# Squeeze-and-excitation scaling of a 256 x 256 x 384 image: more rows kept in SBUF, another row layout, small loads at the end of the first pass, a quartered first store, and an early table load

## Chip, cores, metric

One core of a Trainium2 chip. Times are device microseconds (us) of one execution; medians over several executions are given. Kernel before: 315.64 us median of 4 runs (315.46 to 316.08).

## The reference

```python
def reference(x, w_down, w_up):          # x: 1 x 256 x 256 x 384, bf16
    s = x.mean(axis=(1, 2))
    s = _sigmoid(_silu(s @ w_down) @ w_up)
    return x * s[:, None, None, :]
```

The scale of every channel depends on all pixels, so x has to be read once for the mean and be there a second time for the product. x is 50.3 MB and SBUF is smaller: what doesn't fit is loaded twice. Below, "row" is one pixel's 384 channels, 768 bytes in each of 128 partitions, that is 98,304 bytes in all; x has 512 rows per partition.

## The kernel before

```python
    R = 16; budget = 207_500; misc_bytes = 5 * 1024        # [defaults written in; cut]
    S = min(T, (budget - misc_bytes) // slot_bytes)         # 16 slots of 16 rows
    xv = xf.rearrange("(t p r) c -> t p (r c)", p=P, r=R)   # a tile is one contiguous block
    # ... [cut]
    for t in range(T):                                      # pass 1
        xt = slots[t % S]
        nc.sync.dma_start(out=xt[:, :], in_=xv[t])
        accumulate_rows(xt, R)          # one matmul with a column of ones per row, into sum_ps
    # mean_sb (ACT) -> psT (PE) -> sT_b (DVE) -> z_ps (PE) -> sig_sb (ACT) -> silu_sb (DVE)
    # -> z2_ps (PE) -> s_bc (ACT): the scale row in all partitions   [cut]
    # pass 2: for each tile in the queue, the resident ones first:
    nc.vector.tensor_tensor(out=x3, in0=x3, in1=s_bc[...], op=ALU.mult)   # in place
    nc.scalar.dma_start(out=dst, in_=xs_)
    nc.sync.dma_start(out=slots[v][:, :], in_=xv[nt])       # the slot's next tile, if any left
```

Loads go through the SP queue, stores through the ACT queue. The tile framework puts in the waits: a load into a slot waits for those stores that read the bytes it overwrites.

Of the kernel before, what the change touches and what calls it, by code (L numbers as in the profile page):

```python
# [10 lines left out]
BF16 = mybir.dt.bfloat16  # L11
ACT = mybir.ActivationFunctionType
ALU = mybir.AluOpType

_D = lambda k, d: type(d)(os.environ.get(k, str(d)))


@with_exitstack
def kernel(
    ctx: ExitStack,  # L20
    tc: tile.TileContext,
    x: bass.AP,
    w_down: bass.AP,
    w_up: bass.AP,
    out: bass.AP,
):
    nc = tc.nc
    P = nc.NUM_PARTITIONS

    B, H, W, C = x.shape  # L30
    Cr = w_down.shape[1]
    NROWS = B * H * W
    assert C % P == 0
    KC = C // P

    xf = x.rearrange("b h w c -> (b h w) c")
    of = out.rearrange("b h w c -> (b h w) c")

    ROW_BYTES = C * 2

    R = _D("DEV_R", 16)
    budget = _D("DEV_BUDGET", 207_500)
    misc_bytes = 5 * 1024
    p1_load_eng = _D("DEV_P1L", "sync")
    p2_load_eng = _D("DEV_P2L", "sync")
    p2_store_eng = _D("DEV_P2ST", "scalar")
    tail_split = _D("DEV_TAIL", 1)
    first_split = _D("DEV_FIRST", 1)
    nfree = _D("DEV_NFREE", 0)

    rows_pp = NROWS // P
    while R > 1 and rows_pp % R != 0:
        R //= 2
    T = rows_pp // R
    slot_bytes = R * ROW_BYTES
    S = min(T, (budget - misc_bytes) // slot_bytes)
    assert S >= 2, f"{S=}"
    n_res = S - nfree
    res_start = T - n_res
    if os.environ.get("DEV_VERBOSE", "1"):  # L60
        print(f"[dev] R={R} T={T} S={S} n_res={n_res} slot_bytes={slot_bytes} traffic_MB={(2*rows_pp+R*res_start)*ROW_BYTES*P/1e6:.1f}")

    xv = xf.rearrange("(t p r) c -> t p (r c)", p=P, r=R)
    ov = of.rearrange("(t p r) c -> t p (r c)", p=P, r=R)

    _engs = {"sync": nc.sync, "scalar": nc.scalar, "gpsimd": nc.gpsimd}

    def eng(name, i=0):
        if name in _engs:
            return _engs[name]  # L70
        if name == "alt":
            return nc.sync if i % 2 == 0 else nc.scalar
        if name == "alt3":
            return [nc.sync, nc.scalar, nc.gpsimd][i % 3]
        raise ValueError(name)

    consts = ctx.enter_context(tc.tile_pool(name="consts", bufs=1))
    small = ctx.enter_context(tc.tile_pool(name="small", bufs=1))
    slots_pool = ctx.enter_context(tc.tile_pool(name="slots", bufs=1))
    psum = ctx.enter_context(tc.tile_pool(name="psum", bufs=1, space=bass.MemoryType.PSUM))  # L80

    ones_bf = consts.tile([P, 1], BF16)
    nc.vector.memset(ones_bf[:], 1.0)  # L83
    ones_row = consts.tile([1, P], BF16)
    nc.vector.memset(ones_row[:], 1.0)  # L85

    wd_bf = consts.tile([P, KC, Cr], BF16)
    nc.scalar.dma_start(wd_bf[:], w_down.rearrange("(k p) j -> p k j", p=P))
    wu_bf = consts.tile([Cr, C], BF16)
    nc.scalar.dma_start(wu_bf[:], w_up)  # L90

    slots = [
        slots_pool.tile([P, R * C], BF16, tag=f"slot{v}", name=f"slot{v}") for v in range(S)
    ]

    sum_ps = psum.tile([1, C], FP32)
    total_mm = rows_pp
    mm_state = {"i": 0}

    def accumulate_rows(xt_ap, nrows):  # L100
        for r in range(nrows):
            i = mm_state["i"]
            nc.tensor.matmul(  # L103
                sum_ps[:, :],
                lhsT=ones_bf[:, 0:1],
                rhs=xt_ap[:, r * C : (r + 1) * C],
                start=(i == 0),
                stop=(i == total_mm - 1),
            )
            mm_state["i"] = i + 1  # L110

    for t in range(T):
        xt = slots[t % S]
        eng(p1_load_eng, t).dma_start(out=xt[:, :], in_=xv[t])  # L114
        accumulate_rows(xt, R)
    assert mm_state["i"] == total_mm

    mean_sb = small.tile([1, C], BF16)
    nc.scalar.activation(mean_sb[:], sum_ps[:], ACT.Copy, scale=1.0 / float(NROWS))  # L119
    psT = psum.tile([P, KC * P], FP32)  # L120
    for k in range(KC):
        nc.tensor.matmul(  # L122
            psT[:, k * P : (k + 1) * P],
            lhsT=mean_sb[0:1, k * P : (k + 1) * P],
            rhs=ones_row[0:1, 0:P],
            start=True,
            stop=True,
        )
    sT_b = small.tile([P, KC * P], BF16)
    nc.vector.tensor_copy(sT_b[:], psT[:])  # L130
    z_ps = psum.tile([Cr, P], FP32)
    for k in range(KC):
        nc.tensor.matmul(  # L133
            z_ps[:, :],
            lhsT=wd_bf[:, k, :],
            rhs=sT_b[:, k * P : (k + 1) * P],
            start=(k == 0),
            stop=(k == KC - 1),
        )
    sig_sb = small.tile([Cr, P], BF16)  # L140
    nc.scalar.activation(sig_sb[:], z_ps[:], ACT.Sigmoid)  # L141
    silu_sb = small.tile([Cr, P], BF16)
    nc.vector.tensor_mul(silu_sb[:], z_ps[:], sig_sb[:])  # L143
    z2_ps = psum.tile([P, C], FP32)
    nc.tensor.matmul(  # L145
        z2_ps[:, :], lhsT=silu_sb[:, :], rhs=wu_bf[:, :], start=True, stop=True
    )
    s_bc = small.tile([P, C], BF16)
    nc.scalar.activation(s_bc[:], z2_ps[:], ACT.Sigmoid)  # L149

    store_state = {"i": 0}

    def scale_and_store(xt, dst, parts=1):
        assert R % parts == 0
        rp = R // parts
        for q in range(parts):
            xs_ = xt[:, q * rp * C : (q + 1) * rp * C]
            x3 = xs_.rearrange("p (r c) -> p r c", c=C)
            nc.vector.tensor_tensor(  # L159
                out=x3,  # L160
                in0=x3,
                in1=s_bc[:, None, :].to_broadcast([P, rp, C]),
                op=ALU.mult,
            )
            eng(p2_store_eng, store_state["i"]).dma_start(  # L165
                out=dst[:, q * rp * C : (q + 1) * rp * C], in_=xs_
            )
            store_state["i"] += 1

    pending = []  # L170
    load_i = 0
    reload = list(range(res_start))
    free_slots = [v for v in range(S) if not (T - 1 - ((T - 1 - v) % S)) >= res_start]
    last_occ = {}
    for t in range(T):
        last_occ[t % S] = t
    free_slots = [v for v in range(S) if last_occ[v] < res_start]
    order = []
    rq = 0
    for v in free_slots:  # L180
        if rq < len(reload):
            tt = reload[rq]
            rq += 1
            eng(p2_load_eng, load_i).dma_start(out=slots[v][:, :], in_=xv[tt])
            load_i += 1
            pending.append((tt, v))
    resident = sorted((t, v) for v, t in last_occ.items() if t >= res_start)
    queue = list(resident) + list(pending)
    pending = []
    qi = 0  # L190
    while qi < len(queue):
        tt, v = queue[qi]
        qi += 1
        is_last = (qi == len(queue)) and rq >= len(reload)
        parts = 1
        if qi == 1:
            parts = first_split
        if is_last or (rq >= len(reload) and qi > len(queue) - 1):
            parts = tail_split
        scale_and_store(slots[v], ov[tt], parts=parts)  # L200
        if rq < len(reload):
            nt = reload[rq]
            rq += 1
            eng(p2_load_eng, load_i).dma_start(out=slots[v][:, :], in_=xv[nt])
            load_i += 1
            queue.append((nt, v))


# [28 lines left out]
```

## Time and profile before

| | before |
|---|---|
| time | 315.64 us |
| HBM read / written | 75.53 / 50.33 MB |
| DMA rate when full | 426 GB/s in pass 1, 430 in pass 2 |
| last load landed to first store's bytes | 123.5 to 134.0 us |
| VectorE, TensorE busy | 34%, 29% |

VectorE and TensorE are far from full. What bounds the kernel, and the lines that show it, stand in the prediction.

### The profile page before, as it was taken

The numbers are of one execution on the slowest core, as the hardware profiler recorded it, in microseconds if no ns is written. First come the engines' busy times: TensorE is split into PE (matmuls) and PEld (weight loads), VectorE is DVE, ScalarE is ACT, GpSimd is POOL, SyncE is SP. The second block draws the span as 40 slices with busy tenths as digits, with TensorE's granted clock in tenths as the row PEclk, the third lists the DMA queues.
The fourth block names the chain that finished last, engine by engine and source line by source line (L and its number), as shares of the span: only waits on it lengthen the run. The fifth ranks groups of instructions, "written<-read, shape, count | busy, mean of one in ns | idle before, by whom it ended". The sixth has DMA issues, their size and how long they took to land.

```text
span 314.0 us, 1303 instructions
## 1 busy us (share of the span) xinstructions
PE 91.7 (29%) x519; PEld 44.0 (14%) x519; DVE 106.5 (34%) x36; ACT 3.8 (1%) x5; POOL 0.2 (0%) x4
## 2 busy tenths in 40 slices
PE   0977577777777777200000000000000000000000
PEld 0433233333333333000000000000000000000000
DVE  0000000000000000599999999994444444000000
ACT  1000000000000000300000000000000000000000
POOL 0000000000000000000000000000000000000000
PEclk9999999999999999655555555555555555555555
DMA  7999999999999994099999999999999999999997
GB/s 284 425 426 423 427 424 426 423 427 426 426 425 427 426 426 184 0 376 343 431 427 429 431 434 431 429 427 429 429 434 431 429 427 431 428 434 431 429 427 307
DMA packets 11962, 125.95 MB, mean 401 GB/s; under 512 B 1692, under 2 KB 1716, under 8 KB 1716
## 3 DMA queue, kind: packets, MB, share of 16 engines
q1 hardware_dynamic: 6912, 75.50, 57.3%
q10 hardware_dynamic: 5044, 50.37, 38.0%
q8 instruction: 4, 0.07, 0.1%
q14 instruction: 2, 0.02, 0.0%
HBM read 75.53 MB, written 50.33 MB: 401 GB/s over the span
## 4 chain that ended last, share of the span: by engine, by line
DMA 76%; DVE 6%; PE 1%; ACT 0%; issue 0%; SPq 0%; ACTq 0%; DVEq 0%
DMA slot<-in_x_dram 38%; DMA out_dram<-slot 34%; DVE slot L159 5%; DMA wd_bf<-in_w_down_dram 5%; PE sum_ps L103 1%; DVE sT_b L130 0%; PE z_ps L145 0%; ACT s_bc L149 0%; ACT mean_sb L119 0%; SPq L114 0%; PE psT L122 0%; PE z_ps L133 0%; DVE silu_sb L143 0%; ACT sig_sb L141 0%; ACTq L165 0%
## 5 line engine op out<-in xcount | busy, mean ns | idle before, releaser
L159 DVE TENSOR_TENSOR slot<-slot,s_bc 128x6144 bf16<-128x6144 bf16 x32 | 105.4, 3357 | 29.7 <-DMA slot<-in_x_dram 28.6
L103 PE MATMUL sum_ps<-slot,ones_bf 128*1 128x384 bf16 x512 | 90.5, 332 | 35.8 <-DMA slot<-in_x_dram 35.8
L103 PEld LDWEIGHTS <-ones_bf 128*1 128x1 bf16 x512 | 43.5, 85 | 82.4 <-issue 44.9
L130 DVE CAST sT_b<-psT 128x384 bf16<-128x384 f32 x1 | 0.6, 559 | 126.2 <-PE psT L122 126.2
L119 ACT ACTIVATE mean_sb<-sum_ps 1x384 bf16<-1x384 f32 x1 | 0.5, 480 | 123.1 <-PE sum_ps L103 123.1
L119 ACT ACT_TABLE_LOAD x1 | 1.3, 1283 | 2.0 <-issue 2.0
L141 ACT ACT_TABLE_LOAD x1 | 1.3, 1283 | 0.0
L145 PE MATMUL z_ps<-wu_bf,silu_sb 24*128 24x384 bf16 x1 | 0.5, 496 | 0.7 <-DVE silu_sb L143 0.7
L143 DVE TENSOR_TENSOR silu_sb<-z_ps,sig_sb 24x128 bf16<-24x128 f32 x1 | 0.3, 278 | 0.7 <-ACT sig_sb L141 0.7
L133 PE MATMUL z_ps<-sT_b,wd_bf 128*24 128x128 bf16 x3 | 0.3, 217 | 0.7 <-DVE sT_b L130 0.7
L122 PE MATMUL psT<-ones_row,mean_sb 1*128 1x128 bf16 x3 | 0.3, 218 | 0.6 <-ACT mean_sb L119 0.6
L149 ACT ACTIVATE s_bc<-z_ps 128x384 bf16<-128x384 f32 x1 | 0.5, 491 | 0.9 <-PE z_ps L145 0.9
L133 PEld LDWEIGHTS <-wd_bf 128*24 128x24 bf16 x3 | 0.2, 90 | 0.7 <-issue 0.6
L83 DVE MEMSET ones_bf<- 128x1 bf16 x1 | 0.1, 59 | 0.8 <-PEq L221 0.8
L122 PEld LDWEIGHTS <-mean_sb 1*128 1x128 bf16 x3 | 0.2, 93 | 1.0 <-ACT mean_sb L119 1.0
L141 ACT ACTIVATE sig_sb<-z_ps 24x128 bf16<-24x128 f32 x1 | 0.3, 267 | 0.1
L145 PEld LDWEIGHTS <-silu_sb 24*128 24x128 bf16 x1 | 0.1, 98 | 0.8 <-DVE silu_sb L143 0.8
L85 DVE MEMSET ones_row<- 1x128 bf16 x1 | 0.2, 165 | 0.0
L221 POOL MEMSET const-bfloat16-1.0<- 128x1 bf16 x1 | 0.1, 102 | 0.0
L221 POOL MEMSET const-uint8-127<- 128x1 uint8 x1 | 0.1, 102 | 0.0
L221 POOL MEMSET const-float32-0.0<- 128x1 f32 x1 | 0.1, 99 | 0.2 <-issue 0.2
L221 POOL MEMSET const-float32-1.0<- 128x1 f32 x1 | 0.1, 99 | 0.0
## 6 DMA issues: line engine op xcount, KB each, us to landing
slot<-in_x_dram SPq DMA_DIRECT2D x48, 1536.0 KB, 25.5
out_dram<-slot ACTq DMA_DIRECT2D x32, 1536.0 KB, 29.0
wd_bf<-in_w_down_dram ACTq DMA_DIRECT2D x1, 18.0 KB, 14.4
wu_bf<-in_w_up_dram ACTq DMA_DIRECT2D x1, 18.0 KB
```

The source lines that it names most:

```text
L85: nc.vector.memset(ones_row[:], 1.0)
L103: nc.tensor.matmul(sum_ps[:, :], lhsT=ones_bf[:, 0:1], rhs=xt_ap[:, r * C : (r + 1) * C], start=(i == 0), stop=(i == total_mm - 1),)
L119: nc.scalar.activation(mean_sb[:], sum_ps[:], ACT.Copy, scale=1.0 / float(NROWS))
L122: nc.tensor.matmul(psT[:, k * P : (k + 1) * P], lhsT=mean_sb[0:1, k * P : (k + 1) * P], rhs=ones_row[0:1, 0:P], start=True, stop=True,)
L130: nc.vector.tensor_copy(sT_b[:], psT[:])
L133: nc.tensor.matmul(z_ps[:, :], lhsT=wd_bf[:, k, :], rhs=sT_b[:, k * P : (k + 1) * P], start=(k == 0), stop=(k == KC - 1),)
L141: nc.scalar.activation(sig_sb[:], z_ps[:], ACT.Sigmoid)
L143: nc.vector.tensor_mul(silu_sb[:], z_ps[:], sig_sb[:])
L145: nc.tensor.matmul(z2_ps[:, :], lhsT=silu_sb[:, :], rhs=wu_bf[:, :], start=True, stop=True)
L149: nc.scalar.activation(s_bc[:], z2_ps[:], ACT.Sigmoid)
L159: nc.vector.tensor_tensor(out=x3, in0=x3, in1=s_bc[:, None, :].to_broadcast([P, rp, C]), op=ALU.mult,)
L221: nc = _bacc.Bacc("TRN2", target_bir_lowering=False, num_devices=1)
```

## The change

Its intent: keep more of x in SBUF (18 slots of 16 rows and one of 3, so that 221 rows and not 256 are loaded twice), and shorten the gap between the passes from both sides. The core of the diff:

```diff
-    budget = _D("DEV_BUDGET", 207_500)
-    misc_bytes = 5 * 1024
+    budget = _D("DEV_BUDGET", 228224)
+    misc_bytes = _D("DEV_MISC", 4224)
-    first_split = _D("DEV_FIRST", 1)
+    first_split = _D("DEV_FIRST", 4)
+    slot_rows = [R] * n_full + ([extra_rows] if extra_rows else [])    # 18 x 16, 3
+    reload_tiles = [8] + [R] * nfr + [rem - 8]                         # 8, 13 x 16, 5
-    xv = xf.rearrange("(t p r) c -> t p (r c)", p=P, r=R)
+    xpp = xf.rearrange("(p r) c -> p (r c)", p=P)     # a partition owns 512 rows in sequence
+    if prewarm:
+        warm = consts.tile([1, 8], BF16)
+        nc.vector.memset(warm[:], 0.0)
+        nc.scalar.activation(warm[:], warm[:], ACT.Sigmoid)
+        if k == len(tiles) - 1:                       # pass 1, how a tile's load is cut
+            cut = [nr] if nr < 15 else [4, 4, 4, 2, 1]
+        elif k >= len(tiles) - 3:
+            cut = [4, 4, 4, 4]
+        for pi, rt in enumerate(pending_reload):      # pass 2, after a slot's store
+            if rt["nrows"] <= slot_rows[v]:
+                xr = slots[v][:, 0 : rt["nrows"] * C]
+                eng(p2_load_eng, load_i).dma_start(out=xr, in_=xpp[...])
-    nc = _bacc.Bacc("TRN2", target_bir_lowering=False, num_devices=1)
+    nc = _bacc.Bacc("TRN2", target_bir_lowering=False, num_devices=1, dynamic_dma_scratch_size=512)
```

The first tile to be loaded again has 8 rows, and it goes into rows 0 to 7 of slot 0, the slot whose multiply and store are made in four pieces of 4 rows.

More of the change, by code (lines that the diff above doesn't have):

```diff
@@ L32 @@
     NROWS = B * H * W
+    assert NROWS % P == 0
     assert C % P == 0
@@ L39 @@
     ROW_BYTES = C * 2
+    rows_pp = NROWS // P
     R = _D("DEV_R", 16)
-    budget = _D("DEV_BUDGET", 207_500)
-    misc_bytes = 5 * 1024
+    budget = _D("DEV_BUDGET", 228224)
+    misc_bytes = _D("DEV_MISC", 4224)
     p1_load_eng = _D("DEV_P1L", "sync")
@@ L47 @@
     tail_split = _D("DEV_TAIL", 1)
-    first_split = _D("DEV_FIRST", 1)
-    nfree = _D("DEV_NFREE", 0)
-    rows_pp = NROWS // P
-    while R > 1 and rows_pp % R != 0:
-        R //= 2
-    T = rows_pp // R
-    slot_bytes = R * ROW_BYTES
-    S = min(T, (budget - misc_bytes) // slot_bytes)
-    assert S >= 2, f"{S=}"
-    n_res = S - nfree
-    res_start = T - n_res
+    first_split = _D("DEV_FIRST", 4)
+    prewarm = _D("DEV_PREWARM", 1)
+    use_extra = _D("DEV_EXTRA", 1)
+    avail = budget - misc_bytes
+    n_full = min(avail // (R * ROW_BYTES), rows_pp // R)
+    extra_rows = 0
+    if use_extra:
+        extra_rows = (avail - n_full * R * ROW_BYTES) // ROW_BYTES
+        extra_rows = min(extra_rows, R - 1, rows_pp - n_full * R)
+        if extra_rows < 1:
+            extra_rows = 0
+    slot_rows = [R] * n_full + ([extra_rows] if extra_rows else [])
+    S = len(slot_rows)
+    res_rows = sum(slot_rows)
+    assert res_rows <= rows_pp
+    reload_rows = rows_pp - res_rows
+    reload_tiles = []
+    nfr = reload_rows // R
+    rem = reload_rows - nfr * R
+    reload_tiles = [8] + [R] * nfr + [rem - 8]
+    assert rem > 8 and sum(reload_tiles) == reload_rows
+    tiles = []
+    row = 0
+    rr_slot = 0
+    for k, nr in enumerate(reload_tiles):
+        if nr <= 0:
+            continue
+        if nr < R and extra_rows and nr <= extra_rows:
+            v = n_full
+        else:
+            v = rr_slot % n_full
+            rr_slot += 1
+        tiles.append(dict(row=row, nrows=nr, resident=False, slot=v))
+        row += nr
+    for v in range(S):
+        nr = slot_rows[v]
+        tiles.append(dict(row=row, nrows=nr, resident=True, slot=v))
+        row += nr
+    assert row == rows_pp
     if os.environ.get("DEV_VERBOSE", "1"):
-        print(f"[dev] R={R} T={T} S={S} n_res={n_res} slot_bytes={slot_bytes} traffic_MB={(2*rows_pp+R*res_start)*ROW_BYTES*P/1e6:.1f}")
-    xv = xf.rearrange("(t p r) c -> t p (r c)", p=P, r=R)
-    ov = of.rearrange("(t p r) c -> t p (r c)", p=P, r=R)
+        print(f"[dev] R={R} S={S} slot_rows={slot_rows} res_rows={res_rows}/{rows_pp} reload_tiles={reload_tiles} traffic_MB={(2*rows_pp+reload_rows)*ROW_BYTES*P/1e6:.2f}")
+    xpp = xf.rearrange("(p r) c -> p (r c)", p=P)
+    opp = of.rearrange("(p r) c -> p (r c)", p=P)
     _engs = {"sync": nc.sync, "scalar": nc.scalar, "gpsimd": nc.gpsimd}
@@ L90 @@
     nc.scalar.dma_start(wu_bf[:], w_up)
+    if prewarm:
+        warm = consts.tile([1, 8], BF16)
+        nc.vector.memset(warm[:], 0.0)
+        nc.scalar.activation(warm[:], warm[:], ACT.Sigmoid)
     slots = [
-        slots_pool.tile([P, R * C], BF16, tag=f"slot{v}", name=f"slot{v}") for v in range(S)
+        slots_pool.tile([P, slot_rows[v] * C], BF16, tag=f"slot{v}", name=f"slot{v}")
+        for v in range(S)
     ]
@@ L110, in accumulate_rows @@
             mm_state["i"] = i + 1
-    for t in range(T):
-        xt = slots[t % S]
-        eng(p1_load_eng, t).dma_start(out=xt[:, :], in_=xv[t])
-        accumulate_rows(xt, R)
+    for k, t in enumerate(tiles):
+        nr = t["nrows"]
+        cut = [nr]
+        if k == len(tiles) - 1:
+            cut = [nr] if nr < 15 else [4, 4, 4, 2, 1]
+        elif k >= len(tiles) - 3:
+            cut = [4, 4, 4, 4]
+        assert sum(cut) == nr
+        r0 = 0
+        for cr in cut:
+            xt = slots[t["slot"]][:, r0 * C : (r0 + cr) * C]
+            eng(p1_load_eng, k).dma_start(
+                out=xt,
+                in_=xpp[:, (t["row"] + r0) * C : (t["row"] + r0 + cr) * C],
+            )
+            accumulate_rows(xt, cr)
+            r0 += cr
     assert mm_state["i"] == total_mm
@@ L151, with scale_and_store @@
     store_state = {"i": 0}
-    def scale_and_store(xt, dst, parts=1):
-        assert R % parts == 0
-        rp = R // parts
+    def scale_and_store(xt, nrows, dst, parts=1):
+        parts = max(1, min(parts, nrows))
+        base = nrows // parts
+        extra = nrows - base * parts
+        r0 = 0
         for q in range(parts):
-            xs_ = xt[:, q * rp * C : (q + 1) * rp * C]
+            rp = base + (1 if q < extra else 0)
+            if rp == 0:
+                continue
+            xs_ = xt[:, r0 * C : (r0 + rp) * C]
             x3 = xs_.rearrange("p (r c) -> p r c", c=C)
@@ L165, in scale_and_store @@
             eng(p2_store_eng, store_state["i"]).dma_start(
-                out=dst[:, q * rp * C : (q + 1) * rp * C], in_=xs_
+                out=dst[:, r0 * C : (r0 + rp) * C], in_=xs_
             )
             store_state["i"] += 1
-    pending = []
-    load_i = 0
-    reload = list(range(res_start))
-    free_slots = [v for v in range(S) if not (T - 1 - ((T - 1 - v) % S)) >= res_start]
-    last_occ = {}
-    for t in range(T):
-        last_occ[t % S] = t
-    free_slots = [v for v in range(S) if last_occ[v] < res_start]
@@ L178 @@
-    order = []
-    rq = 0
-    for v in free_slots:
-        if rq < len(reload):
-            tt = reload[rq]
-            rq += 1
-            eng(p2_load_eng, load_i).dma_start(out=slots[v][:, :], in_=xv[tt])
-            load_i += 1
-            pending.append((tt, v))
-    resident = sorted((t, v) for v, t in last_occ.items() if t >= res_start)
-    queue = list(resident) + list(pending)
-    pending = []
+            r0 += rp
+    resident = [t for t in tiles if t["resident"]]
+    reload = [t for t in tiles if not t["resident"]]
@@ L190 @@
+    queue = [(t, t["slot"]) for t in resident]
+    pending_reload = list(reload)
+    load_i = 0
     qi = 0
+    total = len(tiles)
+    n_done = 0
     while qi < len(queue):
-        tt, v = queue[qi]
+        t, v = queue[qi]
         qi += 1
-        is_last = (qi == len(queue)) and rq >= len(reload)
+        n_done += 1
+        is_last = n_done == total
         parts = 1
-        if qi == 1:
+        if qi <= 1:
             parts = first_split
-        if is_last or (rq >= len(reload) and qi > len(queue) - 1):
+        if is_last:
@@ L199 @@
             parts = tail_split
-        scale_and_store(slots[v], ov[tt], parts=parts)
-        if rq < len(reload):
-            nt = reload[rq]
-            rq += 1
-            eng(p2_load_eng, load_i).dma_start(out=slots[v][:, :], in_=xv[nt])
-            load_i += 1
-            queue.append((nt, v))
+        nr = t["nrows"]
+        xt = slots[v][:, 0 : nr * C]
+        scale_and_store(xt, nr, opp[:, t["row"] * C : (t["row"] + nr) * C], parts=parts)
+        for pi, rt in enumerate(pending_reload):
+            if rt["nrows"] <= slot_rows[v]:
+                pending_reload.pop(pi)
+                xr = slots[v][:, 0 : rt["nrows"] * C]
+                eng(p2_load_eng, load_i).dma_start(
+                    out=xr, in_=xpp[:, rt["row"] * C : (rt["row"] + rt["nrows"]) * C]
+                )
+                load_i += 1
+                queue.append((rt, v))
+                break
@@ L210 @@
+    assert not pending_reload, pending_reload
 _INS = ['x', 'w_down', 'w_up']
```

## The prediction

> **What bounds the kernel now.** The kernel walks x twice: pass 1 loads all 32 tiles of 1536 KB and sums them over the pixels on TensorE, a short chain turns the sums into the scale row s_bc, and pass 2 multiplies by it and stores; the last 16 tiles stay in SBUF and the first 16 are loaded again. I read first the busy share of the 40 slices, then the DMA totals:
>
> ```profile
> DMA  7999999999999994099999999999999999999997
> GB/s 284 425 426 423 427 424 426 423 427 426 426 425 427 426 426 184 0 376 343 431 427 429 431 434 431 429 427 429 429 434 431 429 427 431 428 434 431 429 427 307
> DMA packets 11962, 125.95 MB, mean 401 GB/s; under 512 B 1692, under 2 KB 1716, under 8 KB 1716
> ```
>
> The DMA engines are full everywhere but in three places: the first slice, the slices around 0 between the passes, and two slices just after. So time goes when bytes go, or when those holes shrink. Second, the stretch view, cut where the rate changes (columns: stretch, length, busy of PE, PEld, DVE, ACT, POOL, granted clock, DMA share, GB/s):
>
> ```profile
> 120.00:120.50 0.50, 0.50 (x4) 0.25 (x3) 0.00 (x0) 0.00 (x0) 0.00 (x0) 1.00 0.99 418
> 120.50:121.00 0.50, 0.50 (x5) 0.25 (x3) 0.00 (x0) 0.00 (x0) 0.00 (x0) 1.00 0.71 270
> 121.00:122.00 1.00, 1.00 (x9) 0.52 (x7) 0.00 (x0) 0.00 (x0) 0.00 (x0) 1.00 0.26 111
> 122.00:123.00 1.00, 0.63 (x4) 0.23 (x3) 0.00 (x0) 0.00 (x0) 0.00 (x0) 1.00 0.09 37
> 123.00:134.00 11.00, 3.92 (x23) 1.75 (x22) 4.92 (x4) 2.52 (x4) 0.00 (x0) 0.75 0.00 0
> 134.00:138.00 4.00, 0.00 (x0) 0.00 (x0) 4.00 (x2) 0.00 (x0) 0.00 (x0) 0.50 1.00 418
> 138.00:141.00 3.00, 0.00 (x0) 0.00 (x0) 3.00 (x2) 0.00 (x0) 0.00 (x0) 0.50 1.12 426
> 141.00:147.00 6.00, 0.00 (x0) 0.00 (x0) 6.00 (x3) 0.00 (x0) 0.00 (x0) 0.50 0.94 291
> 147.00:200.00 53.00, 0.00 (x0) 0.00 (x0) 53.00 (x17) 0.00 (x0) 0.00 (x0) 0.50 1.01 430
> ```
>
> Full rate ends near 121; then a few of the 16 DMA engines are still behind (share 0.26, then 0.09, one or two engines); from 123 to 134 nothing moves; stores begin at 134.0, and once loads join them a dip to 291 GB/s costs 6 x (430 - 291) / 430 = 1.9 us. After that 430 GB/s to the end. Third, the chain of work that ended last, in order of time (start, length, what), for the hole itself:
>
> ```profile
> 123.55 2.77 PE sum_ps L103 x16
> ...
> 126.35 0.49 ACT mean_sb L119
> ...
> 128.23 0.28 ACT sig_sb L141
> ...
> 129.40 0.50 ACT s_bc L149
> 129.90 0.02 issue
> 129.92 13.18 DVE slot L159 x4
> ```
>
> Between landing and first store lie 16 matmuls, 2.8 us; mean to scale row, 3.6 us; one multiply, 3.36 us; and 0.7 us from the issue of the store (133.31) to its first bytes (134.0). The end is no place to gain: VectorE makes its last multiply at 260.58, and the stores behind it drain at 430 GB/s for another 48 us.
>
> **What the Trainium skill says.** (1) "DMA: Bandwidth & Descriptors", section "Where 436 GB/s comes from", puts the ceiling of the 16 DMA engines at 435 GB/s; the 426 and 430 here agree, so no better queueing raises the plateau, only fewer bytes help. (2) "SBUF — State Buffer", section "SBUF size: 192, 224, or 256?", gives 224 KiB per partition, about 208 KiB after a reserve of 16 KiB for descriptors that software generates. Kernel before budgets 207,500 B; the change shrinks that reserve to 512 B and budgets 228,224. The page's DMA queues are hardware-dynamic ones and instruction ones, so the reserve serves nothing here; the trace shows nothing against it. (3) The first page again, section "Latency and other measured facts": copies of 128 partitions x 16 KiB lose rate when the row pitch in HBM is a large power of two, 207 GB/s per direction at 512 KiB against 214 at full, 164 at 2 MiB. No run so far shows this: the kernel before reads contiguous tiles.
>
> **The change, part by part.**
>
> *More kept in SBUF.* 228,224 - 4,224 = 224,000 B hold 18 slots of 12,288 B (before 16) and 2,816 B over, so one more slot of 3 rows. Resident are 18 x 16 + 3 = 291 rows per partition of 512, and 221 are loaded again in place of 256. 35 rows x 768 B x 128 partitions = 3.44 MB; at 430 GB/s that is 8.0 us. All of it lies on the bound resource, so it counts in full: -8.0 us.
>
> *The last loads of pass 1 cut small.* The last two full tiles come in pieces of 4 rows, the last piece has 3. After the last landing there are 3 matmuls and not 16: the 16 took 2.77 us, about 0.17 us each, so some 0.6 us, -2.2 us. The pieces before it land every 0.9 us and need 0.7 us of TensorE, so none pile up. The lagging DMA engines are not helped: each piece still needs all 16. Smaller packets cost: in the packet records 12,288 B take 460 ns and 768 B 36 ns; a line through them gives 7.7 ns plus 0.0368 ns per byte, so 3,072 B take 121 ns, and four of them 483 ns instead of 460. For 35 rows so cut that is 0.4 us, and for the split store 0.2: +0.6 us.
>
> *First multiply and store in four.* The first store can leave after a quarter of a multiply. A 128x6144 one takes 3.36 us, of which 6144 elements at 2 x 0.96 per ns are 3.2, so a quarter takes an estimated 0.95 us. Measured from s_bc ready, bytes start at 0.95 + 0.7 = 1.7 us rather than 4.05. But what comes next? Four quarters keep VectorE till 3.8, the next full multiply till 7.2, and the second tile's bytes start at 7.9. The first tile's bytes are through at 1.7 + 3.8 = 5.5. The first load of pass 2 waits for that store's landing (0.9 us after its bytes, as 137.7 to 138.6 before) and needs about 1.3 us to first bytes (as at the kernel's start, 0.73 to 2.0): 7.7. So a hole opens from 5.5 to 7.7. Before, the first tile's bytes were through at 4.05 + 3.7 = 7.7 and the second's ready at 7.4. Both kernels have moved one tile at 7.7 us: the head start of 2.3 us is given back, 0 us net.
>
> *Sigmoid's table loaded early.* The table load before sig_sb ran from 126.84 to 128.12, while z_ps came at 128.21: it was hidden by 0.1 us. 0 us.
>
> *Layout.* Each partition now owns 512 consecutive rows, so the 128 runs of one DMA lie 512 x 768 B = 384 KiB apart. Runs are still 12,288 B, so the packets stay the same size. 384 KiB is three times a power of two and smaller than the skill's mildest case of 3%; I book 0.2%, +0.5 us.
>
> Sum: 315.6 - 8.0 - 2.2 + 0.6 + 0.5 = 306.5 us.
>
> **The rivals.** *A: the pitch bites.* Streams 384 KiB apart might share HBM channels. For it: the skill's table, in which 512 KiB costs 3%; DMA engines in step at such pitches are just what this layout makes. Against it: pass 1 only reads, and the factor 3 spreads addresses. At 3% on 290 us the loss is 9 us and the kernel stands at 314, the same; at 1%, 309. *B: the quartered store does pay.* If the dip after 141 comes from stores and loads meeting with a backlog, then an early, lightly loaded start may remove it, or the load may arrive sooner than 7.7: up to 2.3 us more, 304. Against it stands the count above: VectorE delivers 1.57 MB in 3.36 us, 468 GB/s, too little more than 430 to refill a hole. *C: full slots or new waits.* Loads in flight at once are eight (the chain of waits goes in steps of 29.45 us, eight tiles of 3.68), and eight pieces of 4 rows hold only 7.4 us of work, so a late landing could starve the queue at the end of pass 1. The piece's wait is on a landing 8 DMAs back, and 2.3 us of lag plus 1.3 us of start still fit in 7.4: I give it at most 1 us, 307.5.
>
> **Range and chances.** The 8.0 and 2.2 us are counts on a bound stage, known to perhaps 0.5 us. B pulls to 303.5, A to 311 or, at a full 3%, to 314. So 306.5, range 303.5 to 311.0. Faster by over 2% means below 309.3; only A at more than 1% prevents that, which I give about one in five. Slower needs a pitch loss of 6%: 3%.
>
> **What would show it.** Right: bytes read fall by 3.44 MB; the plateau stays at 424 to 431 GB/s in both passes; three matmuls end the sums within 0.7 us of the last landing; the DMA share drops near 0 for about 2 us, beginning some 4 us after the first store's bytes start; the table load is gone from the hole, yet mean to scale row still takes 3.6 us. Wrong: 12,288 B packets well over 460 ns or a plateau below 420 (A); no second hole after the first store (B); a falling rate before the last landing by more than the 2 us of lag there now (C). The prediction fails mainly if pitch matters more than the odd factor lets me hope.

## The result, and the profile after

303.03 us median (302.82 to 303.38, 8 runs) against 315.69 us (315.34 to 316.22, 13 runs). The ratio is 0.9598, 95% interval 0.9589 to 0.9608; a ratio here is the mean time of one kernel's runs over that of the other's of the same rounds, so not quite the ratio of the medians. Executions over 1.5% slower than the fastest of the same kernel are left out of the means. The direction was right, the size was not: 12.7 us were gained where 9.1 had been booked, and 303.03 lies below the range of 303.5 to 311.0.

The page of the kernel after, its DMA totals and two of its lines on DMA issues (size of each, median time from issue to landing):

```profile
DMA packets 13691, 122.52 MB, mean 407 GB/s; under 512 B 1884, under 2 KB 1908, under 8 KB 4468
...
out_dram<-slot ACTq DMA_DIRECT2D x30, 1536.0 KB, 26.7
...
out_dram<-slot ACTq DMA_DIRECT2D x4, 384.0 KB, 2.6
```

125.95 - 122.52 = 3.43 MB are gone, as counted. The quarters' stores land 2.6 us after issue, where whole tiles take 26.7: next to nothing is queued ahead of them.

Its stretch view from the scale row on (columns as in the prediction):

```profile
128.00:129.20 1.20, 0.00 (x0) 0.00 (x0) 1.20 (x3) 0.00 (x0) 0.00 (x0) 0.50 0.00 0
129.20:131.00 1.80, 0.00 (x0) 0.00 (x0) 1.80 (x4) 0.00 (x0) 0.00 (x0) 0.50 0.97 386
131.00:133.00 2.00, 0.00 (x0) 0.00 (x0) 2.00 (x1) 0.00 (x0) 0.00 (x0) 0.50 0.99 390
133.00:134.50 1.50, 0.00 (x0) 0.00 (x0) 1.50 (x2) 0.00 (x0) 0.00 (x0) 0.50 1.01 270
134.50:142.50 8.00, 0.00 (x0) 0.00 (x0) 8.00 (x3) 0.00 (x0) 0.00 (x0) 0.50 1.01 430
142.50:147.50 5.00, 0.00 (x0) 0.00 (x0) 5.00 (x3) 0.00 (x0) 0.00 (x0) 0.50 1.01 329
147.50:200.00 52.50, 0.00 (x0) 0.00 (x0) 52.50 (x18) 0.00 (x0) 0.00 (x0) 0.50 1.01 430
```

The first bytes start at 129.2 and not at 134.0, and **the second hole that the prediction announced is not there**: the DMA share stays at 0.97 to 1.01, where it was to fall near 0 for 2 us from about 133. There are two slow stretches, 270 from 133.0 and 329 from 142.5, but busy ones. Worked out as the prediction does for its dip of 1.9 us, they cost 0.6 and 1.2 us: in all hardly less than before.

Its chain of work that ended last, at the gap (start, length, what):

```profile
122.58 1.37 PE sum_ps L140 x7
...
123.98 0.49 ACT mean_sb L169
...
126.87 0.50 ACT s_bc L199
127.37 0.02 issue
127.39 13.44 DVE slot L214 x8
```

Sums end at 123.95 rather than 126.32, the scale row at 127.37 rather than 129.90.

Why there is no hole: the SP queue's part of the order of time after the scale row (start, length, what), first of the kernel before, then of the kernel after.

```profile
138.60 29.83 SPq L204 DMA_DIRECT2D slot<-in_x_dram  x5
```

```profile
131.93 12.33 SPq L251 DMA_DIRECT2D slot<-in_x_dram  x3
```

In the kernel after, the first load of pass 2 is issued at 131.93. The four stores are issued at 128.38, 129.25, 130.12 and 130.99; by the trace the *second* lands at 131.78, the third at 132.73, the fourth at 134.00. The load goes out after two stores, because its 8 rows go into rows 0 to 7 of slot 0 and overlap only the first two quarters (the experiments below test this). By the records of single packets its bytes begin at 133.46, just before the quarters' last bytes are through at 133.58; the second tile's stores begin only at 135.54.

### The profile page after: what moved, and what is told of

It is laid out like the page before. It is cut to its first block, busy times and chain, and to the rows that moved or that the text cites. A ratio compares the mean times of both kernels' runs of the same rounds, so it can differ in the third digit from the quotient of the medians.

```text
span 301.3 us, 1326 instructions
## 1 busy us (share of the span) xinstructions
PE 90.7 (30%) x519; PEld 43.6 (14%) x519; DVE 106.5 (35%) x42; ACT 2.7 (1%) x5; POOL 0.2 (0%) x4
## 2 busy tenths in 40 slices
DMA packets 13691, 122.52 MB, mean 407 GB/s; under 512 B 1884, under 2 KB 1908, under 8 KB 4468
## 4 chain that ended last, share of the span: by engine, by line
DMA 54%; DVE 19%; issue 8%; PE 1%; ACT 0%; DVEq 0%; SPq 0%
DMA slot<-in_x_dram 43%; DVE slot L214 19%; DMA out_dram<-slot 10%; DMA wd_bf<-in_w_down_dram 1%; PE sum_ps L140 0%; DVE sT_b L180 0%; ACT s_bc L199 0%; ACT mean_sb L169 0%; PE psT L172 0%; PE z_ps L195 0%; PE z_ps L183 0%; DVE silu_sb L193 0%; ACT sig_sb L191 0%; DVEq L214 0%; SPq L251 0%
## 5 line engine op out<-in xcount | busy, mean ns | idle before, releaser
L214 DVE TENSOR_TENSOR slot<-slot,s_bc 128x6144 bf16<-128x6144 bf16 (+4 forms) x37 | 105.5, 2925 | 14.7 <-DMA slot<-in_x_dram 13.8
## 6 DMA issues: line engine op xcount, KB each, us to landing
slot<-in_x_dram SPq DMA_DIRECT2D x42, 1536.0 KB, 26.7
out_dram<-slot ACTq DMA_DIRECT2D x30, 1536.0 KB, 26.7
out_dram<-slot ACTq DMA_DIRECT2D x1, 480.0 KB, 26.7
```

The source lines that it names most:

```text
L214: nc.vector.tensor_tensor(out=x3, in0=x3, in1=s_bc[:, None, :].to_broadcast([P, rp, C]), op=ALU.mult,)
```

## The experiments

Each changes one thing in the kernel after (one in the kernel before). Differences in us are taken from ratios, times 315.66; the 95% interval of one ratio is about 0.4 us to each side, where nothing else is said.

**Swap the first two loads of pass 2**, so that 16 rows come first and overlap all four quarters:

```diff
-    pending_reload = list(reload)
+    pending_reload = [reload[1], reload[0]] + list(reload[2:])
```

> The changed kernel with one swap in the order of the second pass: the first tile to be loaded again (into slot 0) is one of 16 rows, the one of 8 rows goes into slot 1. Nothing else moves, bytes are the same. Theory (the small first load): the 8-row load overlaps only the first two quarters of the slot, so it waits for two stores and fills the hole that the prediction counted; with 16 rows it must wait for all four, the hole of about 2.2 us at 4 us after the first store's bytes opens, and the time is 303.0 + 2.2 = 305.2 us. Rival (the early start pays by itself, the dip where loads join stores is lighter because it meets no backlog): no change, 303.0 us.

Measured: 305.00 us (304.84 to 305.19), ratio 0.9662, so 2.0 us slower than the kernel after. Its load is issued at 133.97, and its stretch view shows the hole:

```profile
133.97 0.33 SPq L251 DMA_DIRECT2D slot<-in_x_dram  x1
```

```profile
129.00:131.00 2.00, 0.00 (x0) 0.00 (x0) 2.00 (x4) 0.00 (x0) 0.00 (x0) 0.50 0.82 326
131.00:133.00 2.00, 0.00 (x0) 0.00 (x0) 2.00 (x2) 0.00 (x0) 0.00 (x0) 0.50 0.99 398
133.00:135.00 2.00, 0.00 (x0) 0.00 (x0) 2.00 (x2) 0.00 (x0) 0.00 (x0) 0.50 0.38 100
135.00:137.00 2.00, 0.00 (x0) 0.00 (x0) 2.00 (x1) 0.00 (x0) 0.00 (x0) 0.50 0.86 264
```

A share of 0.38 from 133 to 135, where the kernel after had about 1. By the packet records the quarters' bytes end at 133.47 and the load's begin at 134.93. That is the prediction's hole, only shorter: from 6.0 to 7.5 us after the scale row, 1.5 us, where 5.5 to 7.7 had been counted.

**Same load, other rows.** Is it the size of the first load, or what it waits for? The 8 rows go into rows 8 to 15 of slot 0:

```diff
+        o = t.get("off", 0)
-        xt = slots[v][:, 0 : nr * C]
+        xt = slots[v][:, o * C : (o + nr) * C]
-                xr = slots[v][:, 0 : rt["nrows"] * C]
+                rt["off"] = o = R - rt["nrows"] if load_i == 0 else 0
+                xr = slots[v][:, o * C : (o + rt["nrows"]) * C]
```

> The changed kernel; the 8 rows loaded first in the second pass go into rows 8 to 15 of slot 0 and not into rows 0 to 7, so they overlap the last two quarters. Same size, same order, same bytes. Theory (what counts is which stores the load must wait for): it waits for the fourth store as the 16-row load of the swap run did, the hole of some 2 us opens, 305.0 us. Rival (what counts is the size of the first load): 303.0 us.

Measured: 304.74 us (304.31 to 304.85), ratio 0.9651, 1.7 us slower. The load is issued at 133.96, the same moment as in the swap, though it has 8 rows:

```profile
133.96 12.95 SPq L253 DMA_DIRECT2D slot<-in_x_dram  x3
```

```profile
133.00:135.00 2.00, 0.00 (x0) 0.00 (x0) 2.00 (x2) 0.00 (x0) 0.00 (x0) 0.50 0.35 83
```

So the wait decides: shown by two kernels with loads of different size and the same wait, and by two with the same size and different waits.

**First multiply and store whole**, and **both edits**:

```diff
-    first_split = _D("DEV_FIRST", 4)
+    first_split = _D("DEV_FIRST", 1)
```

> The changed kernel with the first multiply and store whole, the 8-row first load kept. Theory: the first store's bytes start 4.05 us after the scale row instead of 1.7, nothing gives it back, so 303.0 + 2.4 = 305.4 us. The prediction's own account (split store worth 0 net): 303.0 us.

> Both edits: first store whole, and 16 rows loaded first. Theory: split store and small first load pay only together, so this equals each edit alone, 305.3 us within 0.4. If the small load and the split each paid by itself, the costs would add: 307.5 us.

Measured: 305.48 us (ratio 0.9676, +2.5) for the whole first store, 305.77 (0.9687, +2.8) for both. Together with the swap (+2.0) and the kernel after (0) that is a table of two by two:

| time against the kernel after | 8 rows first | 16 rows first |
|---|---|---|
| first store in quarters | 0 | +2.0 |
| first store whole | +2.5 | +2.8 |

With 16 rows first the quarters are worth 0.8 us; with 8 rows first, 2.5. The 8-row load alone, with the first store whole, is worth 0.3. Neither has most of its effect without the other. The expectation that each alone would cost as much as both was off by the 0.8.

**Contiguous tiles again**, all else as after:

```diff
-    xpp = xf.rearrange("(p r) c -> p (r c)", p=P)
+    def blk(flat, t):
+        b = flat[t["row"] * P : (t["row"] + t["nrows"]) * P, :]
+        return b.rearrange("(p r) c -> p (r c)", p=P)
```

> The changed kernel with each tile a contiguous block of pixels again (as in the kernel before; the 128 runs of one DMA 12 KiB apart, not 384 KiB), same sizes, same order. Theory (the pitch costs nothing): 303.0 us within 0.4, packets of 12,288 B at 460 ns in both. Rival (the pitch costs some): faster by 0.5 us or more, 302.5 or below.

Measured: 303.16 us (302.92 to 303.60), ratio 0.9606; packets of 12,288 B have a median of 461 ns (loads) and 460 ns (stores) in both. The pitch of 384 KiB costs nothing that these runs resolve.

**Last loads of pass 1 uncut:**

```diff
-            cut = [nr] if nr < 15 else [4, 4, 4, 2, 1]
-        elif k >= len(tiles) - 3:
-            cut = [4, 4, 4, 4]
+            cut = [nr]
```

> The changed kernel with the last loads of the first pass uncut: two tiles of 16 rows, then the slot of 3 rows. After the last landing stand most of 16 matmuls and then 3: about 2.6 us after it rather than the 0.7 to 1.4 of the changed kernel, so +1.6; packets of 3,072 B gone from 32 rows, -0.4. Theory: 303.0 + 1.2 = 304.2 us. If small packets cost more than booked, less: 303.5; if they cost nothing, 304.6.

Measured: 304.75 us (304.60 to 304.99), ratio 0.9654, 1.8 us slower, where 1.2 was expected. In its chain the sums end so:

```profile
122.32 3.26 PE sum_ps L140 x19
```

That is 125.58, against 123.95: 1.6 us of the 1.8. Without the small packets the last bytes are there 0.3 us sooner (122.49 against 122.80), but after the last landing stand 2.6 us of matmuls and not 0.7. The cut's net worth was booked at 2.2 - 0.4 = 1.8 in the prediction.

**No early table load:**

```diff
-    prewarm = _D("DEV_PREWARM", 1)
+    prewarm = _D("DEV_PREWARM", 0)
```

> The changed kernel without the early activation that loads Sigmoid's table. Theory: the load hides behind the transposing matmuls and the copy, 303.0 us within 0.3. Rival (it is on the path): up to 1.3 us more, 304.3.

Measured: 302.89 us, ratio 0.9598, the same as the kernel after. The load was hidden.

**The kernel before with 18 slots**, nothing else:

```diff
-    budget = _D("DEV_BUDGET", 207_500)
-    misc_bytes = 5 * 1024
+    budget = _D("DEV_BUDGET", 228224)
+    misc_bytes = 4224
```

(and the smaller descriptor reserve).

> The kernel before with only its SBUF budget changed: 18 slots of 16 rows in place of 16, 14 tiles loaded again in place of 16. 32 rows x 98,304 B = 3.15 MB less at 430 GB/s: 315.7 - 7.3 = 308.4 us within 0.4. If residency were worth less than its bytes (a wait in place of a transfer), more than 309.

Measured: 307.82 us (307.62 to 308.05), ratio 0.9751, a gain of 7.9 us for 32 rows where 7.3 had been worked out from the bytes. Residency is worth its bytes at least. The interval, 7.4 to 8.3 us, leaves the excess barely outside the noise; where it comes from isn't settled.

**A step further in the same direction:** the first load of pass 2 in two pieces of 4 rows, each behind one store, and the second tile's multiply and store in halves.

```diff
+        if qi == 2:
+            parts = 2
+                n0, hs = rt["nrows"], (rt["nrows"] // 2 if load_i == 0 else rt["nrows"])
+                for h in range(0, n0, hs):
+                    # one dma_start for rows h to h + hs
```

> The changed kernel with the mechanism taken a step further: the first load of the second pass in two pieces of 4 rows, each waiting for one store, and the second tile's multiply and store in two halves. Theory: the first loaded bytes come about 1 us earlier, the rate of 390 between first store and first load and the dip to 270 after it fill up; 0.3 to 0.7 us faster, 302.5 us. Rival (the dip belongs to the joining of loads and stores and not to a lack of work): 303.0 us within 0.2.

Measured: 303.94 to 310.70 us in six runs, three of them slow by the rule of 1.5%; the fast ones are at 303.94, 303.99 and 305.51, ratio 0.9646 (0.9627 to 0.9665). Not faster by the expected 0.3 to 0.7 us but 1.5 us slower, and unsteady; why was not found, and its profiled run was a slow one. The last experiment has the extra pieces too, and a fast profile.

**Twelve more rows kept, in PSUM.** Residency being worth its bytes, six of the eight PSUM banks are free if the matmuls of the chain share one. The Trainium skill, "PSUM — Partial Sum Buffer", section "Specifications (TRN2)", gives 4-byte types as the ones that VectorE and ScalarE write to PSUM (no run here tries a narrower one), so VectorE copies pairs of bf16 as int32, by a bitwise "and" of each with itself:

```diff
+    tiles.append(dict(row=row, nrows=KEEP, resident=False, slot=15, kept=True))    # KEEP = 12
+            for b in range(KEEP // 2):                     # pass 1, after that tile's matmuls
+                w = slots[15][:, 2 * b * C : (2 * b + 2) * C].bitcast(mybir.dt.int32)
+                nc.vector.tensor_tensor(
+                    out=keep_ps[b][:, 0:C], in0=w, in1=w, op=ALU.bitwise_and
+                )
+        if n_done == 25:                                   # pass 2: PSUM x s_bc into slot 15
+            # six tensor_tensor, one store of 12 rows
```

> The changed kernel with 12 more rows kept, in six idle banks of PSUM: VectorE copies them there bit by bit during the first pass, and multiplies them from there into slot 15 late in the second, when that slot has been stored. Bytes loaded fall by 12 x 98,304 = 1.18 MB. Theory (residency is worth its bytes wherever it lies): 303.0 - 2.7 = 300.3 us within 0.4. If VectorE's slower reads of PSUM or a new wait shows, 301 or more.

Measured: 300.41 us (300.22 to 301.21), correct, ratio 0.9517, interval 0.9505 to 0.9529: 2.6 us below the kernel after, 2.7 expected. This beats both kernels. Of its groups of instructions by line:

```profile
L172 DVE TENSOR_TENSOR keep<-slot 128x384 int32<-128x384 int32 x6 | 2.9, 561 | 54.7 <-DMA slot<-in_x_dram 54.7
L260 DVE TENSOR_TENSOR slot<-keep,s_bc 128x768 bf16<-128x768 bf16 x6 | 2.9, 550 | 31.3 <-DMA out_dram<-slot 31.3
```

Six copies in pass 1 and six multiplies in pass 2, 2.9 us for each six, on an engine that waits for DMA before both: no cost of them shows in the time. The slower reads of PSUM that the expectation allowed for did not show either: from SBUF the same multiply took 760 ns for 128x1152 and 954 for 128x1536, and 550 for 128x768 from PSUM lies on that line.

**Both together:**

> Both of the last two together: rows kept in PSUM and the pieces. If they add: 303.0 - 2.7 - 0.5 = 299.8 us; if only PSUM counts, 300.3 us.

Measured: 300.09, 300.17, 300.42 and 302.23 us in the fast runs, two slow ones near 305.7; ratio 0.9527 (0.9505 to 0.9548). Nothing over PSUM alone. Its stretch view (the profiled run was fast):

```profile
129.00:131.00 2.00, 0.00 (x0) 0.00 (x0) 2.00 (x4) 0.00 (x0) 0.00 (x0) 0.50 0.82 324
131.00:133.00 2.00, 0.00 (x0) 0.00 (x0) 2.00 (x3) 0.00 (x0) 0.00 (x0) 0.50 1.08 298
133.00:135.00 2.00, 0.00 (x0) 0.00 (x0) 2.00 (x2) 0.00 (x0) 0.00 (x0) 0.50 0.94 356
```

Its first load goes out at 131.02, 0.9 us sooner, and the slow stretch comes sooner as well (298 from 131 to 133, in the kernel after 270 from 133 to 134.5), with the share near 1 both times. In the kernel before it began near 141, between the first load's issue (138.60) and its first bytes (142.2). A slow stretch thus goes with loads joining the stores, and the engines are busy in it: in the kernel after, packets of 3,072 B take 225 ns from 133.0 to 133.5 and about 121 otherwise. The earlier load brings the stretch forward. The second slow stretch of the kernel after is not seen here (427 GB/s from 141 to 145, 426 to 151), and yet the time is no better. Where that was lost again was not found, and what makes the packets slow was not tested.

## Why the prediction was wrong

Its terms against what the runs gave:

| term | booked | measured | from |
|---|---|---|---|
| 35 rows fewer to load | -8.0 | about -7.9 | what is left of 12.7 after the terms below; from the first store's bytes to the end the profiles have 180.0 and 172.1 us; 32 rows alone gave -7.9 |
| cut at the end of pass 1, with its small packets | -1.8 | -1.8 | uncut run |
| first store in quarters, with the small first load | +0.2 | -2.8 | both edits undone |
| layout | +0.5 | -0.2, within the intervals | contiguous tiles |
| early table load | 0 | 0 | run without it |

**The step that failed** is in the part on the first multiply: "The first load of pass 2 waits for that store's landing", and with it "So a hole opens from 5.5 to 7.7" and "the head start of 2.3 us is given back, 0 us net". There is no one store to wait for. The tile is stored in four, and a load waits for those stores only whose bytes it overwrites. The diff had the fact in plain view, a list of loads that begins with 8 and a slice of rows 0 to 7, but the prediction nowhere mentions the 8.

It was right about a kernel without that pairing: the swap run has the hole at the announced place. Even there it was mis-sized: the quarters' bytes end 6.0 us after the scale row and not 5.5, and the load's come 0.96 us after its issue and not 1.3 (a figure taken from the kernel's cold start), so the hole is about 1.5 us and not 2.2, and the split keeps 0.8 us. That the load's issue between them, at 6.5 us, was booked at 6.4 is luck: from the last bytes to the issue it takes 0.5 us, here and in the kernel before (138.08 by the packet records to 138.60), and not 0.9; the prediction had worked out its 137.7 and not read it.

So 2.0 us of this term are the wait that was not there, and 0.8 the hole's length. With the 0.2 for its small packets, the term of the first store missed by 3.0 us. The layout, which cost nothing, adds 0.7; the total missed by 3.5.

**The other points.** Bytes and the plateau of 430 GB/s in pass 2 held. The sums end 0.69 us after the last landing (123.26), as booked; the chain shows 7 matmuls and not 3 because the piece before had landed only 0.7 us earlier. Mean to scale row took 3.4 us, not 3.6, and this varies from run to run: the chain's last matmul took 331 ns at a granted clock of 1.00, in the kernel before 496 at 0.50, and in the PSUM run, where the chain does the same work, 498 again. A quarter's multiply was estimated at 0.95 us and took 954 ns. Packets of 3,072 B were estimated at 121 ns; they took 124 for loads, 121 for stores. Rival A, the pitch, fell: a loss of over 1% had been given about one chance in five, and the sum held 0.5 us for it. Rival B said that the quartered store pays because the dip is lighter or "the load may arrive sooner than 7.7"; the second half of that sentence is what happened, the first is not (the slow stretches cost 1.7 us, before 1.9). It was argued down by VectorE's 468 GB/s, which is true and beside the point: the hole is filled by a load, not by VectorE. Rival C did not show as a starved queue: the rate falls to 395 GB/s from 118 to 121 us, where the small packets are loaded, but the DMA share is 1.03 there.

**Left open:** whether 32 rows gain more than their bytes, and why; the slow stretch when loads join; the unsteady runs with more pieces.

## What to carry to other kernels

When a store is split, look up for each later load which of the pieces it overlaps: the load waits for the last of those and no more, so a split store and a small load into its first pieces work as a pair, and each is worth little alone. In this kernel, whose DMA engines are full, every row kept was worth its bytes at the full rate, and idle PSUM banks could hold rows too. Before booking a new hole, list everything that could fill it, with the exact wait of each.

## What the Trainium skill lacked or had wrong

- "DMA: Bandwidth & Descriptors", section "Latency and other measured facts": its table of HBM row pitches has powers of two from 512 KiB up and two paddings of 4 MiB, nothing smaller and no other multiple. Here a pitch of 384 KiB, three times a power of two, cost nothing: ratio to before 0.9598 with it, 0.9606 without, packets at 460 to 461 ns.
- "SBUF — State Buffer", section "SBUF size: 192, 224, or 256?": it leaves about 208 KiB after the reserve for software-generated descriptors, and does not say that the reserve can be given up. Here, where the page of the profile shows hardware-dynamic and instruction queues only, a reserve of 512 B was enough: slots of 221,184 B (18 of 16 rows) fit and ran correctly in the kernel before, a gain of 7.9 us, and of 223,488 B in the kernel after.
- No page read tells that transfers run slowly for some us when loads join a stream of stores: 291 GB/s over 6 us before, 270 over 1.5 us and 329 over 5 us after, with a DMA share of 0.94 to 1.01.
- "VectorE: DVE Perf Modes", section "The perf-mode tier table (the rule you actually need)", gives tensor_tensor 2x for bf16 in SBUF, but only 1x with any operand in PSUM. Here a bf16 multiply with one operand in PSUM was not slower: 128x768 took 550 ns, in line with 760 and 954 ns for 128x1152 and 128x1536 from SBUF.
